# A gated mix of linear attention and a dense squared-ReLU block on one core: low weight parts kept in DRAM, sums moved between engines, and a new table of slots

## The chip, the cores and the metric

The kernel runs on one core of one Trainium2 chip. A core has a matrix engine (TensorE; PE for its matmuls and PEld for its weight loads in the profile), VectorE (DVE), ScalarE (ACT), GpSimd (POOL) and SyncE (SP), which here issues nearly all DMAs. Each engine works through its own instructions in order and waits at semaphores for the others. The metric is device time in microseconds (us). Before the change the median of three runs is 535.49 us (534.55 to 535.69). The profiled execution took 532.88 us, of which 531.1 us lie between its first and its last instruction (the span).

## The reference

`x` is 2048 x 512, in float32. There are 32 heads of 16 features, and the hidden layer of the dense block has 1792 units.

```
g = sigmoid((x * gate_w).sum(-1))
q, k, v = split(x @ wqkv)                      # 32 heads of 16
pq, pk = q @ w_phi[h], k @ w_phi[h]            # per head
phi = concat(softmax(p), softmax(-p))          # 32 features a head, of pq and of pk
kv, z = phi_k^T @ v, phi_k.sum(rows)
a = ((phi_q @ kv) / (phi_q @ z + 1e-6)) @ wo
r = relu(x @ w1 + b1)
b = (r * r) @ w2 + b2
out = g * a + (1 - g) * b
```

## The kernel before

**Precision.** Each large product is made of three matmuls. An operand is split into a high part `hi` (a copy that ScalarE rounds to a shorter format) and a low part `lo = x - hi` (a subtraction, on VectorE or on GpSimd); `mm3` (lines 72 to 75) adds hi.hi, hi.lo and lo.hi in PSUM. So every operand costs a ScalarE copy and a subtraction before TensorE may read it; both are in `split`, where the copy is line 65 and the subtraction line 68.

**Two sweeps.** The rows of `x` are taken in 4 blocks of 512. The first sweep goes through the blocks with hidden chunks 0 to 6 of the dense block, and in the same time makes K and V and sums them into `kv`. The second sweep goes through the blocks again with hidden chunks 7 to 13, and makes Q, the attention's numerator and the output. One step is one chunk for one block: 12 matmuls "up" (`u`) and 12 "down" (`d`), of 128x512 each. The up product runs two steps ahead of the down product (`LAG = 2`). First-sweep results of the dense block go to DRAM (`part`) and are read back in the second sweep.

**K and V by seven products.** A pair is 256 rows. The product of its rows with [K weights | V weights] is made as a 2 x 2 block product in Winograd's form: seven block products instead of eight (`p1` to `p7`), from sums of the left side (`S1` to `S4`, by `rows_make` on GpSimd) and of the right side (`T1` to `T4`, by `sums_make`, line 237, on GpSimd, once for the whole kernel). There are 8 pairs, two in each block. `w_phi` is folded into the K weights (`fold("k")`, small matmuls of 32x32) and into the Q weights (`fold("q")`) before use. Two PSUM banks serve the seven products: `ps_a` holds `X` (p1 + p2) and then `Z` (p5 + p3), `ps_b` holds `Y` (p6, then p7, then p4 in the same bank). VectorE empties them: `t`, `vext` and `k` on line 538, and the features by two reductions and two subtractions, lines 331 to 334, an exponential on ScalarE (336), a sum (339), a reciprocal (341) and a scaling (345). `do_kv` then multiplies the features with V, head by head (line 354), and adds the result to `kvs` by four additions of 17 rows (line 588).

**What sets the order.** The table `steps` is filled by `at(slot, function, ...)`. Slots 2t and 2t + 1 belong to step t, and the first sweep has slots 0 to 55. A scheduling layer then orders each engine's instructions by the order of the program and by its own idea of when their inputs are ready, with a few hints (`high_priority`, `issue_after`). The DMAs of the SP queue are ordered in the same way, and SP waits at each for its buffer.

**The weights of the dense block in the first sweep.** Chunks 0 to 6 are needed in all four blocks, and there is no room to keep them on chip. So each chunk's `w1` and `w2` tile (128x512, 256 KB) is fetched again for each block into one of four staging buffers (`in`), split into `hi` on ScalarE and `lo` on GpSimd (21 + 21 times from block 1 on), and held in one of three buffers each (`fpool`, `NSTR = 3`). The same four staging buffers take the rows of `x` for the gate (`gate_load`).

**The gate.** For each 128 rows VectorE makes a dot product (line 303), ScalarE an exponential of one column (308), and VectorE four small operations (310 to 313).

Of the kernel before, what the change touches and what calls it, by code (L numbers as in the profile page):

```python
# [16 lines left out]
P = 128  # L17
# [7 lines left out]
LAG = 2  # L25
# [10 lines left out]
def tile_gated_mix(ctx: ExitStack, tc: tile.TileContext, xT, xn, wqT, wkT, wphi, wv, wo, w1, b1, w2, b2, gw, out):  # L36
# [72 lines left out]

    def ready(nm, fc, elo=nc.vector):  # L110
# [57 lines left out]
    xkept = dram.tile([NB, NK, 2, P, SB], F32, name="xkept")  # L168
    kvs = const.tile([P, 2 * P], F32, name="kvs")
    nc.gpsimd.memset(kvs, 0.0)  # L170
    vext = [hold.tile([P, H * VW], F32, tag="vz", name=f"vext{i}") for i in range(NV)]
    heads = lambda v: v.rearrange("p (h v) -> p h v", v=VW)
    for v in vext:
        nc.gpsimd.memset(heads(v)[:, :, DH:VW], 1.0)
    zbc = []
# [34 lines left out]
    def raws(*tags):  # L210
        return [wpool.tile([P, 512], F32, tag=tag, name="fold") for tag in tags]

    def foldq_load():
        load_fold("q", wqT, raws("T40l", "T41h", "T41l", "T10h"))
# [17 lines left out]
    def sums_make(kk, early):  # L232
        k1, k2, v1, v2 = st["w", "k"][kk], st["w", "k"][2 + kk], raw["v", kk], raw["v", 2 + kk]
        t1, t4 = [raw.setdefault((op, kk), row()) for op in ("T1", "T4")] if early else (raw["T1", kk], raw["T4", kk])
        raw["T2", kk], raw["T3", kk] = v2, v1
        for o, x, y in ((t1, v1, k1), (v1, v2, v1)) if early else ((v2, v2, t1), (t4, k2, v2)):
            nc.gpsimd.tensor_tensor(o, x, y, ALU.subtract)
# [61 lines left out]
    def gate_dot(n):  # L299
        t = st["xn", n]  # L300
        lg = st["lg", n] = small.tile([P, 1], F32, tag="lg", name="lg")
        with tc.issue_after(st["low"].ins):
            nc.vector.scalar_tensor_tensor(t, t, 1.0, gwb, op0=ALU.mult, op1=ALU.mult, accum_out=lg)

    def gate_chunk(n):
        e = small.tile([P, 1], F32, tag="ge", name="ge")
        with tc.issue_after(st["act"].ins):
            nc.scalar.activation(e, st["lg", n], AF.Exp, scale=-1.0)
        s = slice(n, n + 1)
        nc.vector.tensor_scalar(inv[:, s], e, 1.0, None, ALU.add)  # L310
        nc.vector.reciprocal(e, inv[:, s])
        nc.vector.tensor_scalar(rest[:, s], e, -1.0, 1.0, ALU.mult, ALU.add)
        nc.vector.tensor_scalar(eps[:, s], inv[:, s], 1e-6, None, ALU.mult)
# [36 lines left out]
    def kv_chunk(n, kvps, phi, v):  # L350
        for i in range(NG):
            for j in range(4):
                h = 8 * (i % 4) + 4 * (i // 4) + j
                nc.tensor.matmul(kvps[32 * j:32 * j + VW, 32 * i:32 * i + 32], v[:, h * VW:(h + 1) * VW],
                                 phi[:, 32 * h:32 * h + 32],
                                 start=(n % 2 == 0 and i == 0), stop=(n % 2 == 1),
                                 skip_group_check=True)
# [116 lines left out]
    def start():  # L474
# [12 lines left out]
        st["wphi"], = raws("T40h")  # L487
        nc.sync.dma_start(st["wphi"], wphi)
        load_fold("k", wkT, raws("T30h", "T30l", "T31h", "T31l"))
# [91 lines left out]
    def do_kv(p):  # L581
# [3 lines left out]
        for j in range(4):  # L585
            s = slice(32 * j, 32 * j + VW)
            with tc.high_priority(offset=AHEAD):
                nc.vector.tensor_tensor(kvs[s, :], kvs[s, :], ps[s, :], ALU.add)
# [13 lines left out]
    def kv_done():  # L602
# [3 lines left out]
        for half in range(2):  # L606
            z = hold.tile([P, H * VW], F32, tag="vz", name=f"z{half}")[:, :D]
# [39 lines left out]
    for nm, fc, s in (("w1", 5, 2), ("w2", 3, 2), ("w1", 6, 4), ("w2", 4, 4), ("w2", 5, 6), ("w2", 6, 8)):  # L647
        at(s, fetch, nm, fc)
    for t in range(NFH, NB * NFH):
        for nm, s in (("w1", 2 * t - 5), ("w2", 2 * t - 2)):  # L650
            at(s - 3, fetch, nm, t % NFH)
            at(s, ready_later, nm, t % NFH, nc.gpsimd)

    for kk in range(2):
        for op, s in (("B11", 3), ("B22", 4), ("B21", 5), ("T2", 6), ("T1", 8), ("T3", 9), ("T4", 10)):
            at(s, operand_ready, op, kk)
    for kk in range(2):
        at(3, sums_make, kk, True)
        at(4, sums_make, kk, False)
    for p, made, split_at in ((0, 2, 3), (1, 3, 12), (2, 12, 15), (3, 16, 20), (4, 24, 26), (5, 30, 32), (6, 36, 38), (7, 40, 42)):  # L660
        at(made, rows_make, p)
        at(split_at, rows_ready, p)
    for p in range(NPAIR):
        s = 8.5 + 5.5 * p
        for f, d in ((p1, 0), (p6, 1), (p2, 1), (p5, 3), (p7, 3), (p4, 4), (p3, 4)):
            at(s + d, f, p)
        at(min(s + 7.5, NB * SL - 3), do_kv, p)
    for b in range(NB):
        for c in range(NC):
            s = b * SL + 3 * c - 5 if b else 7 + c  # L670
            at(s, gate_load, b * NC + c)
            at(s + 3 if b else 9 + c, gate_dot, b * NC + c)
            at(s + 5 if b else 10 + c, gate_chunk, b * NC + c)
        at(b * SL + 16, x_save, b)
        if b < NB - 1:
            at((5, 18, 32)[b], x_fetch, b + 1)
            for k in range(NK):
                at((7, 21, 35)[b] + k // 2, x_ready, b + 1, k)
    base = (NB - 1) * SL
    at(3, foldq_load)  # L680
    at(7, fold, "q")
    at(8, foldq_move)
# [8 lines left out]
    at(NB * SL - 3, kv_done)  # L691
# [28 lines left out]
    for t, (sw, b, i) in enumerate(work_list):  # L720
# [31 lines left out]
        for c in range(NC):  # L752
# [68 lines left out]
```

## Time and profile before

| | |
|---|---|
| median of 3 runs | 535.49 us |
| the profiled execution | 532.88 us |
| its span | 531.1 us |
| PE busy (modelled) | 508.8 us |
| DVE busy | 444.4 us |
| ACT busy | 256.6 us |
| POOL busy | 149.6 us |
| moved by DMA | 70.64 MB |
| the last instruction of the first sweep on PE (`kvt`) | at 277.8 us |

A profile lists, for each engine, how long it was busy and what ended its idle time. "Busy" on PE is modelled: a matmul of 128x512 is shown as about 0.39 us long, but the next one starts 0.23 us after it, so overlapping rows hide short idle times. The arrow `<-` in a row of waits names the engine, the output tile and the line that the waiting instruction was released by.

### The profile page before, as it was taken

To read this page: it belongs to the slowest core of one execution; us is meant where nothing else is said; L and a number is where in the kernel's file an instruction comes from. 1 tells how busy PE (TensorE), PEld (TensorE's weight loads), DVE (VectorE), ACT (ScalarE), POOL (GpSimd) and SP (SyncE) were. 2 spreads that over 40 slices of the span, in tenths; PEclk is the share of its full clock that TensorE was granted. 3 is DMA by queue.
4 is the path that set the end of the run, shared out by engine and by line. 5 is a ranking of instruction groups with operands and counts; after the bars stand their busy time and mean duration, and the time that the engine had idled before them with its cause. 6 is when DMAs were issued, how large, how long until landed. Compare 5 with 4: busy or idle time off the path is not lost.

```text
span 531.1 us, 9626 instructions
## 1 busy us (share of the span) xinstructions
PE 508.8 (96%) x3616; PEld 405.3 (76%) x3616; DVE 444.4 (84%) x704; ACT 256.6 (48%) x446; POOL 149.6 (28%) x125
## 2 busy tenths in 40 slices
PE   9969989999979999899989999999999999999997
PEld 5847867787867878678768887878787878788776
DVE  5898999999698997989899979796779777888723
ACT  6646646564526382546464745353534434343530
POOL 4293324542564242123111112121111020211100
PEclk9997999999999999999999999999999999999999
DMA  8859445426443266623267715312226221023112
GB/s 300 296 199 321 136 130 171 157 74 205 136 141 82 80 201 230 238 66 118 83 179 228 236 52 184 97 38 60 76 53 217 65 91 47 11 92 89 35 26 79
DMA packets 44662, 70.64 MB, mean 133 GB/s; under 512 B 7240, under 2 KB 13640, under 8 KB 44616
## 3 DMA queue, kind: packets, MB, share of 16 engines
q1 hardware_dynamic: 44296, 69.63, 40.9%
q8 instruction: 28, 0.46, 0.3%
q10 hardware_dynamic: 288, 0.39, 0.2%
q14 instruction: 18, 0.15, 0.1%
q0 software_dynamic: 32, 0.01, 0.0%
HBM read 45.88 MB, written 17.83 MB: 120 GB/s over the span
## 4 chain that ended last, share of the span: by engine, by line
PE 62%; issue 13%; DVE 11%; POOL 6%; DMA 5%; ACT 1%; SPq 1%; POOLq 0%; DVEq 0%; ACTq 0%
PE d L73 6%; PE d L75 6%; PE d L74 6%; PE u L73 6%; PE u L74 6%; PE u L75 6%; PE q L73 3%; PE q L75 3%; PE att L75 3%; PE att L73 3%; PE q L74 3%; PE att L74 3%; POOL w2l L68 2%; POOL row L256 2%; DMA in<-in_w 2%
## 5 line engine op out<-in xcount | busy, mean ns | idle before, releaser
L435 ACT ACTIVATE r<-u,b1c 128x512 f32<-128x512 f32 x56 | 38.4, 685 | 122.7 <-PE u L75 122.3
L363 POOL TENSOR_TENSOR ez<-e,z 128x512 f32<-128x512 f32 x32 | 41.4, 1313 | 184.5 <-ACT e L336 162.5
L73 PE MATMUL d<-w2h,hh 128*128 128x512 f32 x160 | 63.7, 398 | 0.7 <-DVE row L768 0.7
L68 POOL TENSOR_TENSOR w1l<-in,w1h 128x512 fp32r<-128x512 f32 x21 | 28.5, 1356 | 124.9 <-ACT w1h L65 106.1
L75 PE MATMUL d<-w2h,hl 128*128 128x512 f32 x160 | 63.2, 395 | 0.0
L74 PE MATMUL d<-w2l,hh 128*128 128x512 f32 x160 | 63.0, 393 | 0.0
L75 PE MATMUL u<-xh,w1l 128*128 128x512 f32 x152 | 60.1, 395 | 2.3 <-DVE w1l L68 1.6
L73 PE MATMUL u<-xh,w1h 128*128 128x512 f32 x152 | 60.6, 399 | 1.0 <-ACT w1h L65 0.9
L74 PE MATMUL u<-xl,w1h 128*128 128x512 f32 x152 | 59.8, 393 | 0.0
L68 DVE TENSOR_TENSOR hl<-r,hh 128x512 fp32r<-128x512 f32 x56 | 48.5, 867 | 13.1 <-ACT hh L65 13.0
L336 ACT ACTIVATE e<-e 128x1024 f32<-128x1024 f32 x32 | 33.9, 1059 | 46.6 <-DVE e L334 46.3
L339 DVE TENSOR_REDUCE sm<-e 128x64 f32<-128x1024 f32 x32 | 38.9, 1216 | 20.3 <-ACT e L336 20.2
L387 ACT ACTIVATE phiT<-tb 32x256 f32<-32x256 f32 x64 | 26.5, 413 | 31.6 <-DVE tb L381 30.9
L73 PEld LDWEIGHTS d<-w2h,hh 128*128 128x128 f32 x160 | 30.3, 189 | 7.9 <-DVE row L768 1.2
L75 PEld LDWEIGHTS u<-xh,w1l 128*128 128x128 f32 x152 | 28.8, 190 | 9.5 <-DVE w1l L68 2.0
L65 ACT ACTIVATE hh<-r 128x512 fp32r<-128x512 f32 x56 | 35.3, 630 | 1.4
L436 ACT ACTIVATE r<-r 128x512 f32<-128x512 f32 x56 | 35.2, 628 | 1.2
L73 PEld LDWEIGHTS u<-xh,w1h 128*128 128x128 f32 x152 | 28.7, 189 | 9.3 <-ACT w1h L65 1.8
L75 PEld LDWEIGHTS d<-w2h,hl 128*128 128x128 f32 x160 | 30.4, 190 | 6.7 <-issue 0.4
L68 POOL TENSOR_TENSOR w2l<-in,w2h 128x512 fp32r<-128x512 f32 x21 | 33.1, 1575 | 8.7 <-issue 8.2
L74 PEld LDWEIGHTS d<-w2l,hh 128*128 128x128 f32 x160 | 30.3, 190 | 6.1
L74 PEld LDWEIGHTS u<-xl,w1h 128*128 128x128 f32 x152 | 28.9, 190 | 5.8
(543 smaller groups left out, 1248.9 us busy)
## 6 DMA issues: line engine op xcount, KB each, us to landing
in<-in_w SPq DMA_DIRECT2D x66, 256.0 KB, 2.8
phiT<-tb SPq DMA_DIRECT2D x192, 32.0 KB, 1.8
xin<-in_xT SPq DMA_DIRECT2D x16, 256.0 KB, 4.6
xkept<-xh SPq DMA_DIRECT2D x16, 256.0 KB, 4.0
xkept<-xl SPq DMA_DIRECT2D x16, 256.0 KB, 4.4
in<-in_xn SPq DMA_DIRECT2D x16, 256.0 KB, 2.8
part<-row SPq DMA_DIRECT2D x16, 256.0 KB, 2.1
xh<-xkept SPq DMA_DIRECT2D x16, 256.0 KB, 4.8
```

The source lines that it names most:

```text
L65: i = nc.scalar.activation(hi, src, AF.Copy)
L68: st["low"] = elo.tensor_tensor(lo, src, hi.bitcast(F32), ALU.subtract)
L73: nc.tensor.matmul(o, ah[:, sa], bh[:, sb], start=first, stop=False, **kw)
L74: nc.tensor.matmul(o, ah[:, sa], bl[:, sb], start=False, stop=False, **kw)
L75: return nc.tensor.matmul(o, al[:, sa], bh[:, sb], start=False, stop=last, **kw)
L256: nc.gpsimd.tensor_tensor(o[i], x, y, op)
L336: nc.scalar.activation(ef, ef, AF.Exp)
L339: nc.vector.tensor_reduce(sm, e3, AX.X, ALU.add)
L363: nc.gpsimd.tensor_tensor(ez[:, hs, :], e3[:, hs, :], zbc[half], ALU.mult)
L387: nc.scalar.activation(dst, src, AF.Copy)
L435: nc.scalar.activation(r, ps, AF.Relu, bias=b1c[:, fc:fc + 1])
L436: nc.scalar.activation(r, r, AF.Square)
```

## The change

It has six parts.

1. **Low parts kept.** In block 0 the low part of each `w1` and `w2` chunk is written to DRAM once it is made (`keep`: 14 DMAs of 256 KB). In blocks 1 to 3, `again` fetches the weights as before and reads the low part back straight into its place (42 DMAs of 256 KB); `again_ready` makes only the high part, on ScalarE. The 42 subtractions on GpSimd are gone. The low part's tile is taken when the DMA is issued, two slots before the high part is made.
2. **Right-hand sums** (`sums_make`, 8 subtractions of 128x512) go from GpSimd to VectorE, one slot later.
3. **wq folded in block 1**: `fold("q")` goes from slot 7 to slot 19; its inputs go to `row` tiles and a staging buffer, where they had gone to weight buffers that were still free.
4. **Bank uses respaced**: `p1` starts at slots 8, 13, 20, 25, 30, 35, 40, 46 where it started at 8, 14, 19, 25, 30, 36, 41, 47; `p3` comes before `p4`, which goes one slot further back. `do_kv` is 8 slots after `p1`.
5. **One addition into kvs**: `do_kv`'s matmuls take 32 columns of V instead of 17, so that they fill whole groups of 32 rows, and one addition of 128x256 replaces four of 17x256 (the additional rows are not used). `vext` gets 15 more columns, of zeros at its end.
6. **Gate by blocks**: one chain of exponential and four small operations on 4 columns per block, where there was one on 1 column per 128 rows; the loads and dots have other slots. The writes of `part` in blocks 0 to 2 are put one to two slots later into the program. `rows_make` and `x_fetch` get other slots too.

```
+    def keep(nm, fc):
+        nc.sync.dma_start(lkept[fc, int(nm == "w2")], (up_w if nm == "w1" else down_w)[fc][1].bitcast(F32))
+    def again(nm, fc):
+        fetch(nm, fc)
+        hi, lo = raw[nm, fc, "hl"] = ffn_tiles(nm, fc)
+        nc.sync.dma_start(lo.bitcast(F32), lkept[fc, int(nm == "w2")])
+    def again_ready(nm, fc):
+        hi, lo = raw.pop((nm, fc, "hl"))
+        with tc.issue_after(st["act"].ins):
+            nc.scalar.activation(hi, raw.pop((nm, fc)), AF.Copy)
...
     def foldq_load():
-        load_fold("q", wqT, raws("T40l", "T41h", "T41l", "T10h"))
+        load_fold("q", wqT, [row() for _ in range(NK)])
+        st["wphi"] = load(wphi)
...
-            nc.gpsimd.tensor_tensor(o, x, y, ALU.subtract)
+            nc.vector.tensor_tensor(o, x, y, ALU.subtract)
...
-                nc.tensor.matmul(kvps[32 * j:32 * j + VW, 32 * i:32 * i + 32], v[:, h * VW:(h + 1) * VW],
+                nc.tensor.matmul(kvps[32 * j:32 * j + 32, 32 * i:32 * i + 32], v[:, h * VW:h * VW + 32],
...
-        for j in range(4):
-            s = slice(32 * j, 32 * j + VW)
-            with tc.high_priority(offset=AHEAD):
-                nc.vector.tensor_tensor(kvs[s, :], kvs[s, :], ps[s, :], ALU.add)
+        with tc.high_priority(offset=AHEAD):
+            nc.vector.tensor_tensor(kvs, kvs, ps, ALU.add)
...
+    for fc in range(NFH):
+        at(max(2 * (fc - LAG), 1) + 1, keep, "w1", fc)
+        at(2 * fc + 1, keep, "w2", fc)
     for t in range(NFH, NB * NFH):
-        for nm, s in (("w1", 2 * t - 5), ("w2", 2 * t - 2)):
-            at(s - 3, fetch, nm, t % NFH)
-            at(s, ready_later, nm, t % NFH, nc.gpsimd)
+        at(2 * t - 8, again, "w1", t % NFH)
+        at(2 * t - 6, again_ready, "w1", t % NFH)
+        at(2 * t - 4, again, "w2", t % NFH)
+        at(2 * t - 2, again_ready, "w2", t % NFH)
...
-        for op, s in (("B11", 3), ("B22", 4), ("B21", 5), ("T2", 6), ("T1", 8), ("T3", 9), ("T4", 10)):
+        for op, s in (("B11", 4), ("B22", 5), ("T2", 6), ("B21", 6), ("T1", 7), ("T3", 8), ("T4", 9)):
...
-    for p in range(NPAIR):
-        s = 8.5 + 5.5 * p
-        for f, d in ((p1, 0), (p6, 1), (p2, 1), (p5, 3), (p7, 3), (p4, 4), (p3, 4)):
+    at(16, foldq_load)
+    at(19, fold, "q")
+    at(20, foldq_move)
+    for p, s in enumerate((8, 13.5, 20, 25.2, 30.4, 35.6, 40.8, 46)):
+        for f, d in ((p1, 0), (p6, 1), (p2, 1), (p5, 3), (p7, 3), (p3, 4), (p4, 5)):
             at(s + d, f, p)
-        at(min(s + 7.5, NB * SL - 3), do_kv, p)
+        at(min(s + 8, NB * SL - 2), do_kv, p)
...
+            elif sw == 0 and b < NB - 1:
+                at(2 * t + 3 + c // 2, lambda *a: nc.sync.dma_start(*a), dst, o)
```

The next lines show what the table makes of three places. They are the scheduled rows of one engine; the numbers behind names are tile numbers of each build, and nothing in them is a time.

**VectorE at the start, in step 1**, around the transposes of the folded K weights (`wkin<-foldk`). `w1l` is the low part of a chunk of w1. Before:

```order
L68 TENSOR_TENSOR w1l_231<-in,w1h_230 128x512
L68 TENSOR_TENSOR hl<-r,hh 128x512
L68 TENSOR_TENSOR w2l_255<-in,w2h_254 128x512
L68 TENSOR_TENSOR w1l_359<-in,w1h_358 128x512
L68 TENSOR_TENSOR w2l_363<-in,w2h_362 128x512
L68 TENSOR_TENSOR S0ol_384<-row,S0oh_382 128x512
L68 TENSOR_TENSOR S0ol_385<-row,S0oh_383 128x512
L206 STREAM_TRANSPOSE wkin<-foldk_285 128x4x4x32
L206 STREAM_TRANSPOSE wkin<-foldk_286 128x4x4x32
L206 STREAM_TRANSPOSE wkin<-foldk 128x4x4x32 x2
L68 TENSOR_TENSOR B110l<-wkin,B110h 128x512
```

and with the change:

```order
L68 TENSOR_TENSOR w2l_258<-in,w2h_257 128x512
L68 TENSOR_TENSOR w2l_370<-in,w2h_369 128x512
L68 TENSOR_TENSOR S0ol_377<-row,S0oh_375 128x512
L68 TENSOR_TENSOR S0ol_378<-row,S0oh_376 128x512
L222 STREAM_TRANSPOSE wkin<-foldk_292 128x4x4x32
L222 STREAM_TRANSPOSE wkin<-foldk_293 128x4x4x32
L222 STREAM_TRANSPOSE wkin<-foldk 128x4x4x32 x2
L68 TENSOR_TENSOR w1l_234<-in,w1h_233 128x512
L68 TENSOR_TENSOR w1l_366<-in,w1h_365 128x512
L251 TENSOR_TENSOR row<-wvin,wkin 128x512 x2
L251 TENSOR_TENSOR wvin<-wvin 128x512 x2
```

The low parts of w1 chunks 3 and 4 have moved behind the transposes, and the sums of line 251 now stand in VectorE's queue.

**VectorE at the end of a pair** (pair 4 of 0 to 7). `k` is the bank Y emptied after p4, `mx`, `mn` and `e` read it, and `vext<-kz` empties bank Z after p3, which p1 of the next pair waits for. Before:

```order
L538 TENSOR_TENSOR k_2160<-ky,t_1922 128x512
L331 TENSOR_REDUCE mx<-k_2160 128x32
L332 TENSOR_REDUCE mn<-k_2160 128x32
L333 TENSOR_TENSOR e<-k_2160,mx 128x32x16
L334 TENSOR_TENSOR e<-mn,k_2160 128x32x16
L538 TENSOR_TENSOR vext_113<-kz,t_1965 128x32x16
L339 TENSOR_REDUCE sm<-e 128x64
```

and with the change:

```order
L68 TENSOR_TENSOR xl_0_2129<-xin,xh_0_2128 128x512
L68 TENSOR_TENSOR xl_1_2133<-xin,xh_1_2132 128x512
L555 TENSOR_TENSOR vext_114<-kz,t_1932 128x32x16
L555 TENSOR_TENSOR k_2162<-ky,t_1892 128x512
L68 TENSOR_TENSOR hl<-r,hh 128x512
L347 TENSOR_REDUCE mx<-k_2162 128x32
L348 TENSOR_REDUCE mn<-k_2162 128x32
```

`vext<-kz` has moved from behind the four feature operations to ahead of them and of `k`.

**The SP queue at the start**, from the first DMA behind the V weights (`wvin`) on; `in<-in_w` fetches a weight chunk. Before:

```order
L641 DMA gwb<-in_gw 128x512
L83 DMA in<-in_w 128x512 x2
L182 DMA fold<-in_wqT 128x512 x4
L83 DMA in<-in_w 128x512 x2
L642 DMA b2b<-in_b 128x512
```

and with the change:

```order
L111 DMA lkept<-w2l_200 128x512
L656 DMA gwb<-in_gw 128x512
L83 DMA in<-in_w 128x512 x2
L111 DMA lkept<-w1l_224 128x512
L111 DMA lkept<-w1l_184 128x512
L111 DMA lkept<-w1l_189 128x512
L111 DMA lkept<-w2l_258 128x512
L111 DMA lkept<-w2l_370 128x512
```

The loads of the Q weights are gone from this place and writes of low parts stand there. The first `in<-in_w` goes into the staging buffer of w1 chunk 3, so it is issued once the subtraction `w1l_234` above is done.

More of the change, by code (lines that the diff above doesn't have):

```diff
@@ L168, in tile_gated_mix @@
     xkept = dram.tile([NB, NK, 2, P, SB], F32, name="xkept")
+    lkept = dram.tile([NFH, 2, P, 512], F32, name="lkept")
     kvs = const.tile([P, 2 * P], F32, name="kvs")
     nc.gpsimd.memset(kvs, 0.0)
-    vext = [hold.tile([P, H * VW], F32, tag="vz", name=f"vext{i}") for i in range(NV)]
-    heads = lambda v: v.rearrange("p (h v) -> p h v", v=VW)
+    vext = [hold.tile([P, H * VW + 32 - VW], F32, tag="vz", name=f"vext{i}") for i in range(NV)]
+    heads = lambda v: v[:, :H * VW].rearrange("p (h v) -> p h v", v=VW)
     for v in vext:
         nc.gpsimd.memset(heads(v)[:, :, DH:VW], 1.0)
+        nc.gpsimd.memset(v[:, H * VW:], 0.0)
     zbc = []
@@ L486, in start @@
         fetch("w2", 1)
-        st["wphi"], = raws("T40h")
-        nc.sync.dma_start(st["wphi"], wphi)
-        load_fold("k", wkT, raws("T30h", "T30l", "T31h", "T31l"))
+        t = [wpool.tile([P, 512], F32, tag=tag, name="fold") for tag in ("T40h", "T30h", "T30l", "T31h", "T31l")]
+        st["wphi"] = t[0]
+        nc.sync.dma_start(t[0], wphi)
+        load_fold("k", wkT, t[1:])
         fetch("w1", 4)
```

42 lines of the change are left out of this document (20 added, 22 removed).

## The prediction

> **What bounds the kernel now.** I read the page first.
>
> ```profile
> span 531.1 us, 9626 instructions
> PE 508.8 (96%) x3616; PEld 405.3 (76%) x3616; DVE 444.4 (84%) x704; ACT 256.6 (48%) x446; POOL 149.6 (28%) x125
> ```
>
> TensorE looks full, but its busy time is modelled. So next comes the table of windows, cut at stages: the start, the rest of block 0, blocks 1, 2 and 3 of the first sweep, and the second sweep. The columns after the window are its length and the busy time of PE, PEld, DVE, ACT and POOL, then the granted clock, the DMA share and GB/s.
>
> ```profile
> 0.00:38.10 38.10, 34.57 (x251) 23.56 (x251) 29.26 (x32) 23.64 (x40) 21.26 (x26) 1.00 0.76 260
> 38.10:88.00 49.90, 45.96 (x421) 36.25 (x421) 46.23 (x87) 30.52 (x55) 18.26 (x15) 0.90 0.62 203
> 88.00:150.00 62.00, 59.78 (x505) 48.46 (x504) 55.98 (x91) 30.14 (x52) 27.83 (x23) 1.00 0.46 144
> 150.00:214.00 64.00, 58.79 (x499) 47.06 (x497) 56.86 (x97) 30.26 (x52) 25.46 (x20) 1.00 0.45 150
> 214.00:278.00 64.00, 59.97 (x626) 48.07 (x626) 59.07 (x98) 34.99 (x61) 15.44 (x11) 1.00 0.42 132
> 278.00:531.10 253.10, 249.69 (x1320) 201.89 (x1318) 196.99 (x305) 107.07 (x188) 41.35 (x32) 1.00 0.30 93
> ```
>
> In the second sweep PE has no holes up to the tail, and VectorE is busy 197 of 253 us. In the first sweep VectorE is busy 89 to 93% of every stage behind the start: there the two engines are nearly equal, and PE waits. The view of waits, for PE alone (total us, times, longest), names all of its waits but the one at launch:
>
> ```profile
> PE ky L73 <- DVE vext L538: 4.3, 3, 2.2
> PE kx L73 <- DVE vext L538: 4.2, 3, 1.8
> PE foldq L191 <- ACT r L435: 3.4, 1, 3.4
> PE u L75 <- DVE w1l L68: 1.6, 1, 1.6
> PE kvps L354 <- DVE rest L312: 1.4, 1, 1.4
> PE u L73 <- ACT w1h L65: 0.9, 1, 0.9
> PE d L73 <- DVE row L768: 0.7, 1, 0.7
> PE ky L73 <- DVE rest L312: 0.7, 1, 0.7
> PE u L75 <- POOL w1l L68: 0.6, 1, 0.6
> PE kvt L612 <- DVE kvs L588: 0.2, 1, 0.2
> ```
>
> They add up to 18.0 us. Each of the 14 waits hides a little more, since a matmul is shown 0.39 us long while the next starts 0.23 us after it:
>
> ```profile
> 215.02 0.39 PE L75 MATMUL kx<-B110h,xl 128*128 128x512 f32 x1
> 215.25 0.40 PE L73 MATMUL kx<-B111h,xh 128*128 128x512 f32 x1
> ```
>
> That is 14 x 0.16 = 2.2 us. Then there is the clock:
>
> ```profile
> 40.00:43.00 3.00, 2.45 (x126) 2.12 (x126) 2.63 (x3) 2.94 (x6) 0.93 (x1) 0.50 1.00 369
> 43.00:46.40 3.40, 3.40 (x28) 2.26 (x8) 3.40 (x7) 2.98 (x6) 0.73 (x1) 0.50 0.64 140
> 75.00:80.00 5.00, 4.38 (x13) 3.13 (x14) 5.00 (x12) 1.00 (x3) 2.84 (x2) 0.71 0.42 107
> ```
>
> PE is busy 5.85 us at 0.50, which loses 2.9 us, and 5.0 x 0.29 = 1.45 us go at 75. So what PE loses in the first sweep is 18.0 + 2.2 + 4.35 = 24.6 us. No change of waits alone can gain more.
>
> **The change part by part.** Why is VectorE late? One reason is GpSimd: the first row is a subtraction beside a GpSimd one (last row, second fence), the second the same form 8 us later with GpSimd idle.
>
> ```profile
> 34.67 1.78 DVE L68 TENSOR_TENSOR B210l<-wkin,B210h 128x512 fp32r<-128x512 f32 x1
> 42.46 0.68 DVE L68 TENSOR_TENSOR w1l<-in,w1h 128x512 fp32r<-128x512 f32 x1
> ```
>
> ```profile
> 34.16 1.74 POOL L237 TENSOR_TENSOR wvin<-wvin,row 128x512 f32<-128x512 f32 x1
> ```
>
> So a GpSimd subtraction costs VectorE up to 1.1 us; as others may fall into idle time I take 0.8. (The Trainium skill, "SBUF — State Buffer", section "SBUF: two separate sides", says that the two share a port pair which one of them holds for its whole instruction while the other blocks. By that rule each of the 50 GpSimd subtractions that go could have cost its whole length, 1.74 us in the row above and near 87 us in all, and VectorE would have far more room than I count; the rows show 1.1 us at most, and I hold to them.)
>
> Other rows that the sums need, of the view by lines, and two of the chain of waits (start, us; the Q fold's twin at full clock, and one `do_kv`):
>
> ```profile
> L588 DVE TENSOR_TENSOR kvs<-kvs,kvps 17x256 f32<-17x256 f32 x32 | 13.3, 415 | 0.3
> L206 DVE STREAM_TRANSPOSE wkin<-foldk 128x512 f32<-128x512 f32 x4 | 2.5, 680 | 0.0
> L311 DVE RECIPROCAL ge<-inv 128x1 f32<-128x1 f32 x16 | 2.4, 153 | 0.2
> L354 PEld LDWEIGHTS kvps<-e,vext 128*17 128x17 f32 x1024 | 9.3, 96 | 4.6 <-issue 2.5 <-ACT r L436 1.8 <-ACT w2h L65 0.4
> L400 PEld LDWEIGHTS num<-phiT,kvb 64*32 64x32 f32 x256 | 3.9, 106 | 3.8 <-ACT e L336 1.8 <-issue 1.1
> L191 PEld LDWEIGHTS foldq<-fold 32*32 32x32 f32 x128 | 2.2, 135 | 4.4 <-ACT r L435 3.8 <-issue 0.4
> ```
>
> ```profile
> 17.45 1.83 PE foldk L191 x102
> 112.43 1.20 PE kvps L354 x82
> ```
>
> *The start* (to 46.4 us). ACT stood waiting for the GpSimd sums, its ReLU came late, and the Q fold waited 3.4 us for a PSUM buffer; then the clock fell. Sums on VectorE take 8 x 0.68 = 5.4 us, less than what GpSimd's eight took from it (8 x 0.8 = 6.4), and the fold leaves this place. The waits of 3.4 and 1.6, two restarts (0.3) and the clock (2.9) go: 8.2. New: w1 chunk 3's low part stands behind the four transposes (2.5 us), and its up product may wait. The bounds are 0 and 2.5; I take 0.5, since VectorE reaches the transposes two subtractions sooner. Queued behind it is SP, whose next weight fetch wants that staging buffer. Net -7.7 (-5 to -8.2).
>
> *The rest of block 0.* Lost before: 0.9 + 0.6 + 0.7, three restarts and the clock's 1.45, together 4.15. VectorE's 29.26 + 46.23 = 75.5 us to 88 us become: less 15 GpSimd subtractions x 0.8 = 12, plus 5.4 for the sums, less 2.5 (Q transposes, later), 1.25 (three of four `kvs` additions) and 1.7 (three gate chains of four operations near 0.15): 63.5. PE needs 88 less its losses of 12.4 and less the fold (1.8): 74. As VectorE starts some 6 us in and also waits for inputs, 63.5 of 68 leaves little room: I keep 4 us of stalls in place of 4.15, now for VectorE's features and block ends. Net -0.2 (-4.15 to +4).
>
> *The banks* (pairs 1 to 7): 4.3 + 4.2 + 0.7 and seven restarts, 10.3 us. The worst kind, at 212 us on VectorE:
>
> ```profile
> 209.97 0.69 DVE L303 SCALAR_TENSOR_TENSOR in<-in,gwb 128x512 f32<-128x512 f32 x1 [3.38 <-issue]
> 210.59 0.69 DVE L538 TENSOR_TENSOR k<-ky,t 128x512 f32<-128x512 f32 x1
> 213.71 0.68 DVE L538 TENSOR_TENSOR vext<-kz,t 128x512 f32<-128x512 f32 x1
> ```
>
> The gate's dot held the queue 3.4 us, and bank Z was emptied only 3.1 us after `k`'s start, behind the features. Now `vext<-kz` precedes `k`, and PE has 12 + 6 matmuls x 0.23 = 4.1 us between p3's end and the next p1, where the shortest spacing was 2.8. For Y, p7 to p4 is 30 matmuls (6.9 us), not 12. VectorE also loses work here: per block 2.5 us of `kvs`, 1.7 of gates, some 14 x 0.8 = 11 of GpSimd's holds. I leave 1.5 us of waits, for dots that wait for their rows as here. Net -8.8 (-5 to -10.3).
>
> *The end of the sweep*: 1.4 + 0.2 and two restarts, 1.9. `do_kv` is a slot later, and the second sweep's first low parts still stand before `k`: 1.2 stays, net -0.7 (-1.9 to +1). `kv_done` is two slots later; the z loads and GpSimd's product come before the first numerator, many steps on: nothing, or 2 us at most if VectorE's sum over that product blocks its queue.
>
> *The Q fold in block 1.* Its matmuls count on both sides. It holds both up buffers and both banks until VectorE's transposes are through, behind a pair's features. Bounds: 0 (hidden behind 12 down matmuls, 2.8 us) and 4 (more than the 3.4 it waited before); I take 1.6, nearer the low end as ACT is no longer blocked.
>
> *Weights of 32 columns.* Loads of 17 columns take 96 ns; of 32 columns 106 (`num`), or 135 (`foldq`, at half clock). So 8 bursts x 1.20 x 0.10 = 1.0; bounds 0 and 3.9.
>
> *The clock.* At 75 us it fell behind waits of 0.9 and 0.6 us. One more such dip would cost 1.45; with fewer waits, I take 0.8 (0 to 3). (The Trainium skill, "TensorE: Matmul & The Clock Gate", section "What's actually happening", puts the drop behind an idle window of about 3.4 us. The 3.42 us at the fold agrees; the dip at 75 us does not. By the rule this term would be 0 and the sum 0.8 us better.)
>
> *Low parts by DMA.* On GpSimd they cost PE only the 0.6 above, and VectorE its time; `SPq L83 <- POOL` below is their price on the queue.
>
> ```profile
> SPq L83 <- POOL w1l L68: 70.2, 20, 10.3
> ```
>
> ```profile
> in<-in_w SPq DMA_DIRECT2D x66, 256.0 KB, 2.8
> xh<-xkept SPq DMA_DIRECT2D x16, 256.0 KB, 4.8
> ```
>
> Now SP waits for PE instead: a reread for chunk t is issued once chunk t-3's products are done. Until its own use lie two steps, 48 matmuls or 11.0 us, and landing takes 4.8 us by the nearest row (a reread from DRAM): 6 us to spare. Behind it on SP wait fetches, gate rows and `xkept` writes. The 56 transfers add 14.7 MB to 70.6; with the DMA share at 0.62 and less in the first sweep but for the start, I count nothing.
>
> Sum: -7.7 - 0.2 - 8.8 - 0.7 + 1.6 + 1.0 + 0.8 = -14.0. The span becomes 517.1, the profiled execution 518.9. That execution lies 2.6 us under the median of the runs; taken from the median it gives **521.5 us**.
>
> **The rivals.** (a) *Nearly every wait goes*: block 0 has no VectorE stalls and the clock holds, gain 18 to 24 us, 514.5. For it: GpSimd's holds may be worth more than 0.8 each. Against: 63.5 of 68 in block 0. (b) *The start is crowded*: SP stands some 8 us for w1 chunk 3's low part, then writes, rows of `x` and weights come at once; the window from 40 us already ran at DMA share 1.00 and 369 GB/s, so 256 KB take 0.7 us and 40 such transfers 28 us. If weights come late for two or three steps by 2 to 3 us, 7 go: 528.5. Against: the Q weights' 2 MB in and out leave the start. (c) *Slower: the reread is late in every step*, because SP, in order, is held by a gate row or an x write for more than the 6 us to spare. From 0.7 us a step (14/21) on it outweighs the gain; at 1.5 us over 21 steps it costs 31: 552. For it: gate dots held SP before. Against: those holds came with GpSimd's. (d) *VectorE is not relieved*: GpSimd's holds fell into idle time, the sums add 5.4, and waits stay: 534 to 537.
>
> **How the numbers follow.** Forecast (gain 10 to 18) 0.50, (a) 0.21, (b) 0.18, (c) 0.06, (d) 0.05. The range is 510.5 (just under every loss gone, 510.9) to 531 ((b) in full); (c) and (d) are left out. A difference of 0.2% is what can be told from none; slower takes (c) and 0.02 of (d), the same 0.02, so faster 0.90.
>
> **What would show it.** `foldq` no longer waits near 37 us and the clock stays at 1.0 there; POOL busy falls from 150 to about 75 us (50 subtractions near 1.5); the mean of `hl` on VectorE falls under 0.75; eight `kvs` additions of 128x256 near 0.42 us; waits of kx and ky under 2 us. If PE waits for `w1l<-lkept` or for ACT `w1h`, (b) or (c) holds; if `hl` stays long without GpSimd, (d). The second sweep must stay within 1 us of 253; if not, the reasoning is wrong.

## The result, and the profile after

The changed kernel takes 516.16 us (median of 4 runs, 514.65 to 519.11) where the kernel before takes 535.02 us (4 runs, 533.35 to 535.69): a ratio of 0.9659, 95% interval 0.9608 to 0.9709. The profiled execution took 515.52 us with a span of 513.8 us, so 17.3 us less than the span before. The prediction was 521.5 us, within 510.5 to 531.

The page of the changed kernel, its span and busy times:

```profile
span 513.8 us, 9521 instructions
...
PE 503.5 (98%) x3616; PEld 404.0 (79%) x3616; DVE 404.1 (79%) x640; ACT 254.6 (50%) x434; POOL 73.6 (14%) x77
```

VectorE has lost 40 us of busy time and GpSimd 76. The table of windows, with the cuts of the prediction (length, PE, PEld, DVE, ACT, POOL, granted clock, DMA share, GB/s):

```profile
0.00:38.10 38.10, 35.75 (x258) 25.08 (x259) 26.71 (x39) 25.19 (x44) 10.89 (x21) 1.00 0.91 321
38.10:88.00 49.90, 48.27 (x332) 38.97 (x331) 43.92 (x76) 31.26 (x54) 7.97 (x8) 1.00 0.91 303
88.00:150.00 62.00, 59.21 (x619) 47.59 (x618) 45.86 (x76) 29.68 (x49) 6.49 (x8) 1.00 0.64 208
150.00:214.00 64.00, 64.00 (x647) 52.42 (x646) 52.52 (x84) 36.32 (x59) 6.52 (x8) 1.00 0.64 206
214.00:278.00 64.00, 64.00 (x528) 52.74 (x527) 53.11 (x89) 34.26 (x56) 3.00 (x2) 1.00 0.59 193
```

PE has no hole left in blocks 2 and 3, and the clock stays at 1.00. The view of waits names all that is left on PE but the launch:

```profile
PE u L73 <- DVE wqin L222: 2.3, 1, 2.3
PE u L75 <- DVE w1l L68: 1.4, 1, 1.4
PE kz L73 <- DVE e L350: 1.3, 1, 1.3
...
PE kx L73 <- DVE wqin L222: 0.5, 1, 0.5
PE d L73 <- DVE row L786: 0.2, 1, 0.2
```

That is 5.7 us where it was 18.0. No wait of kx or ky for `vext` is among them, nor one for the rereads. SP now waits for PE and ScalarE, no longer for GpSimd:

```profile
SPq L116 <- PE u L75: 34.0, 14, 5.2
SPq L83 <- ACT w2h L121: 32.1, 16, 4.9
```

The gain lies in the first sweep. The first numerator product of the second sweep starts 17.9 us earlier, and from there to the end both kernels take about the same (209.4 us before, 210.0 us now). The view of the tile `num`, before and then after (shortest, median and longest in ns, then first and last start):

```profile
L400 PE MATMUL num<-phiT,kvb x256: 375/376/401, 321.7 to 513.4; 64*32 64x256 f32 x128
```

```profile
L416 PE MATMUL num<-phiT,kvb x256: 373/376/401, 303.8 to 496.0; 64*32 64x256 f32 x128
```

### The profile page after: what moved, and what is told of

It is laid out like the page before. It is cut to its first block, busy times and chain, and to the rows that moved or that the text cites. A ratio compares the mean times of both kernels' runs of the same rounds, so it can differ in the third digit from the quotient of the medians.

```text
span 513.8 us, 9521 instructions
## 1 busy us (share of the span) xinstructions
PE 503.5 (98%) x3616; PEld 404.0 (79%) x3616; DVE 404.1 (79%) x640; ACT 254.6 (50%) x434; POOL 73.6 (14%) x77
## 2 busy tenths in 40 slices
DMA packets 52869, 85.58 MB, mean 167 GB/s; under 512 B 8152, under 2 KB 14552, under 8 KB 52824
## 4 chain that ended last, share of the span: by engine, by line
PE 82%; DVE 7%; DMA 5%; ACT 4%; issue 1%; SPq 1%; DVEq 0%; ACTq 0%
PE u L73 8%; PE d L73 8%; PE d L74 8%; PE d L75 8%; PE u L75 8%; PE u L74 8%; PE q L73 3%; PE q L75 3%; PE q L74 3%; PE att L73 3%; PE att L75 3%; PE att L74 3%; PE kvps L370 2%; PE num L416 2%; PE ky L73 2%; PE ky L74 2%
## 5 line engine op out<-in xcount | busy, mean ns | idle before, releaser
L73 PE MATMUL d<-w2h,hh 128*128 128x512 f32 x160 | 62.8, 393 | 0.2 <-DVE row L786 0.2
L73 PE MATMUL u<-xh,w1h 128*128 128x512 f32 x152 | 59.9, 394 | 2.5 <-DVE wqin L222 2.3
L68 DVE TENSOR_TENSOR hl<-r,hh 128x512 fp32r<-128x512 f32 x56 | 38.6, 689 | 18.3 <-ACT hh L65 18.3
L73 PEld LDWEIGHTS u<-xh,w1h 128*128 128x128 f32 x152 | 28.5, 188 | 10.5 <-DVE wqin L222 2.8
L65 ACT ACTIVATE hh<-r 128x512 fp32r<-128x512 f32 x56 | 35.3, 631 | 1.6
L73 PEld LDWEIGHTS d<-w2h,hh 128*128 128x128 f32 x160 | 30.0, 188 | 7.5 <-DVE row L786 0.7
L270 POOL TENSOR_TENSOR row<-xin 128x256 f32<-128x256 f32 x16 | 16.0, 1006 | 123.5 <-DVE S4ol L68 32.7
L381 DVE TENSOR_REDUCE dz<-ez 128x64 f32<-128x1024 f32 x16 | 19.4, 1211 | 9.4 <-POOL ez L379 9.3
```

What stands on the lines that cost most here:

```text
L65: i = nc.scalar.activation(hi, src, AF.Copy)
L68: st["low"] = elo.tensor_tensor(lo, src, hi.bitcast(F32), ALU.subtract)
L73: nc.tensor.matmul(o, ah[:, sa], bh[:, sb], start=first, stop=False, **kw)
L381: nc.vector.tensor_reduce(dz, ez, AX.X, ALU.add)
```

## The experiments

Twelve kernels were run, in three groups; the runs of the kernel before were taken on the same chip for each group (medians 532.78, 533.19 and 534.47 us), so the ratio is what compares across groups.

| run | median, us | ratio to before (95%) | profiled span, us |
|---|---|---|---|
| the change | 516.16 | 0.9659 (0.9608 to 0.9709) | 513.8 |
| low parts on GpSimd, old slots | 528.34 | 0.9898 (0.9846 to 0.9951) | 528.0 |
| low parts on VectorE, old slots | 526.32 | 0.9867 (0.9824 to 0.9910) | 525.2 |
| sums on GpSimd | 519.87 | 0.9751 (0.9706 to 0.9797) | 518.1 |
| old bank slots | 517.72 | 0.9712 (0.9666 to 0.9758) | 515.5 |
| 42 more operations on VectorE | 516.83 | 0.9676 (0.9632 to 0.9719) | 515.8 |
| staging held by VectorE | 516.65 | 0.9685 (0.9644 to 0.9725) | 514.5 |
| reread twice | 518.76 | 0.9717 (0.9675 to 0.9759) | 517.8 |
| 17 columns, four additions | 518.17 | 0.9712 (0.9666 to 0.9758) | 514.8 |
| low parts on VectorE, the change's slots | 514.98 | 0.9647 (0.9621 to 0.9672) | 512.9 |
| low parts on GpSimd, the change's slots | 527.31 | 0.9877 (0.9852 to 0.9902) | 526.0 |
| three slots moved | 513.87 | 0.9630 (0.9601 to 0.9658) | 512.2 |
| before, with the rereads alone | 519.83 | 0.9734 (0.9708 to 0.9759) | 517.1 |

**Undoing one part at a time.** First the low parts, back on GpSimd, without stores and rereads:

```
-        at(2 * t - 8, again, "w1", t % NFH)
...
+        for nm, s in (("w1", 2 * t - 5), ("w2", 2 * t - 2)):
+            at(s - 3, fetch, nm, t % NFH)
+            at(s, ready_later, nm, t % NFH, nc.gpsimd)
```

> The changed kernel, but the low parts of the FFN weights of blocks 1 to 3 are again subtracted on GpSimd (42 instructions, with the fetches where the kernel before had them) and are neither stored nor reread; sums, banks, fold and gates stay as changed. Theory (VectorE's time is what was short, and each GpSimd subtraction takes up to 1.1 us, about 0.8, of it): VectorE loses 42 x 0.8 = 34 us, some 11 a block, on top of 46 to 53 busy of 62 to 64; it is full again, SP waits for GpSimd near 70 us again, and PE waits of 4 to 9 us come back: 520 to 526 against the change's 516.2. Rival (the new spacing of the banks did it; GpSimd's holds fell into idle time): 515.5 to 517.5, PE waits still near 6 us.

528.34 us, more than either side expected. This part carries the most: 0.0239 of 535 us is 12.8 us. SP waits for GpSimd again (`w1l` alone 71.8 us), but VectorE is not full: it was busy 46.71 of 62 us in block 1. So the direction was right, and the reason given for it was already in doubt.

The same with `nc.vector` in place of `nc.gpsimd`:

> The changed kernel, but the low parts of blocks 1 to 3 are subtracted on VectorE itself (42 more instructions near 0.68 us), neither stored nor reread. Theory (VectorE's time, whoever takes it): 42 x 0.68 = 28.6 us, some 9.5 a block, so blocks 2 and 3 stand at 62 of 64 us and PE waits 3 to 8 us more: 519 to 524. Rival 1 (it was GpSimd: its slow subtractions held the staging buffers and so SP, and stretched VectorE; any quick engine would do): 515.5 to 517.5. Rival 2 (the DMA traffic of the reread costs something): under 515.

526.32 us, beyond the first theory's range, and nothing like the rivals: another engine in the same slots did not clearly help (1.7 us by the ratio, with intervals that overlap).

The sums back on GpSimd (`nc.gpsimd.tensor_tensor` in `sums_make`):

> The changed kernel, but the eight subtractions that make the right-hand sums in block 0 are on GpSimd again. Theory (ACT waited for them, its ReLU came late, PE waited and the clock fell): ACT waits for GpSimd again for 2 to 4 us near 30 to 40 us, PE loses 2 to 6 us there and perhaps half clock: 518 to 522. Rival (the loss at the start came from the Q fold, which stood behind that ReLU, and the fold has left): within 1 us of 516.2.

The theory holds, with 4.3 us more span (the intervals of the two ratios just overlap). ScalarE's timeline shows it waiting at the high parts of T20 and T21 for GpSimd, with the ReLU's second half (line 452) queued behind the second one:

```profile
36.98 0.63 ACT L65 ACTIVATE T20h<-wvin 128x512 fp32r<-128x512 f32 x1 [1.19 <-POOL wvin L251]
37.52 0.67 ACT L451 ACTIVATE r<-u,b1c 128x512 f32<-128x512 f32 x1
40.38 0.63 ACT L65 ACTIVATE T21h<-wvin 128x512 fp32r<-128x512 f32 x1 [2.18 <-POOL wvin L251]
40.91 0.61 ACT L452 ACTIVATE r<-r 128x512 f32<-128x512 f32 x1
```

`w1h` is queued behind that, and PE waited 2.6 us for it (`PE u L73 <- ACT w1h L65: 2.6, 1, 2.6` in the waits). With the sums on VectorE that wait is not there.

The old table of bank slots:

> The changed kernel, but the pairs' products, do_kv and the left-hand sums stand in the slots of the kernel before (p4 ahead of p3, one start every 5.5 slots, do_kv 7.5 slots behind). Theory (spacing and relief share the 10.3 us of bank waits): kx and ky wait for vext again, with a VectorE that is less busy 0.5 to 1.5 us each in place of 1.5 to 2.2: 3 to 7 us, 519 to 523. Rival 1 (the relief of VectorE did it alone): under 1.5 us, 516 to 517.7. Rival 2 (spacing did it alone): all 10 us come back, 526.

The two measures differ. The median, 517.72 us, stands at the edge of rival 1, but the kernel before was faster in this group, and by the ratio the old slots cost 2.8 us (0.0053 of 535), near the theory's lower bound of 3. The intervals of the ratios overlap, and the span is 1.7 us longer. The waits speak for rival 1: PE waited once for `vext`, 0.8 us:

```profile
PE kx L73 <- DVE vext L555: 0.8, 1, 0.8
```

So the respacing, on which the prediction had leaned for the banks, is worth some 2 to 3 us once the low parts are off GpSimd, which these runs cannot tell from nothing.

**What did the low parts cost?** Two additions to the changed kernel part VectorE's time from its hold on the staging buffers. The first adds time only:

```
+            nc.vector.tensor_reduce(junk, hi.bitcast(F32).rearrange("p (h f) -> p h f", f=DH), AX.X, ALU.max)
```

> The changed kernel, rereads and all, with 42 added reductions on VectorE (128x512, near 0.68 us each) that read the high part of a chunk once ScalarE has made it; the staging buffers are not touched by them, and what they write is not used. Theory 1 (VectorE's own time is what the low parts cost): as with the low parts on VectorE, 8 to 12 us more than the change, a ratio to the kernel before of 0.980 to 0.990, with PE waits for VectorE near 10 us in the first sweep. Theory 2 (what cost was the hold: a staging buffer stays taken until the low part is made, SP waits, and the weights and rows behind it come late): at most 3 us more, a ratio of 0.966 to 0.971.

The second holds the staging buffer and takes next to no time:

```
+            nc.vector.tensor_tensor(junk, t[:, :1], hi[:, :1].bitcast(F32), ALU.subtract)
```

> The changed kernel, rereads and all, with 42 added subtractions of 128x1 on VectorE (0.06 to 0.15 us each, some 4 us in all) that read the staged chunk and its high part, so that the staging buffer stays taken until VectorE has come to them; what they write is not used. Theory 1 (VectorE's own time): at most 3 us more than the change, a ratio to the kernel before of 0.966 to 0.971. Theory 2 (the hold of the staging buffers, and SP with them): SP waits for VectorE some 60 us, and 8 to 12 us more, a ratio of 0.980 to 0.990.

Neither costs anything that these runs can tell. With the added reductions (42 near 0.67 us) VectorE is busy 429.7 us in place of 404.1, and the ratio is 0.9676, 0.9 us more; PE's waits add up to 7.7 us in the profiled execution, against 5.7. So VectorE's busy time, taken alone, is not what is short. The hold gives 0.9685; but SP waited only 31 us at these subtractions, not 60, so it was a weaker hold than meant.

That left the slots. The next two runs take the slots of the change for fetch and split, without DRAM, first on VectorE:

```
+        at(2 * t - 8, fetch, "w1", t % NFH)
+        at(2 * t - 6, ready_later, "w1", t % NFH)
+        at(2 * t - 4, fetch, "w2", t % NFH)
+        at(2 * t - 2, ready_later, "w2", t % NFH)
```

> As the run with the low parts on VectorE, no stores, no rereads, but each chunk is fetched and split in the slots of the change: w1 at 2t-8 and 2t-6, w2 at 2t-4 and 2t-2, so that it lies two slots in a staging buffer, not three. Two chunks a step then take 2 of the 4 staging buffers and not 3, with the gate's rows beside them. Theory (neither VectorE's time nor its touch of the buffer cost anything by itself; what cost 11 us was that staging was full and SP, in order, late with all that stands behind it): SP's waits for VectorE's low parts fall from 97 us to under 50, and the ratio to the kernel before is 0.966 to 0.975. Rival (what counts is that a product has to wait for a low part made in VectorE's queue, or that all three costs come together): 0.982 to 0.990, as before.

and then on GpSimd (`ready_later, ..., nc.gpsimd`):

> The same slots, with the low parts on GpSimd. Theory (full staging): the time falls with SP's waits, ratio 0.968 to 0.978, some 2 us behind VectorE's version, as GpSimd's subtractions of 1.4 to 1.7 us hold the buffers longer. Rival (GpSimd itself, by what it takes from VectorE): stays at 0.985 to 0.995.

VectorE's version is as fast as the change, with nothing stored or reread (70.89 MB moved, not 85.58). GpSimd's is 12.3 us slower in the same group of runs, inside its rival's range, and the engine of 42 subtractions is the only difference in what is written. But the reason in the expectation fell: SP waits longer than with the old slots, and still the time is low. The queue's waits of VectorE's version, then of GpSimd's:

```profile
SPq L83 <- DVE w2l L68: 81.7, 26, 15.4
SPq L83 <- DVE w1l L68: 24.1, 23, 6.8
```

```profile
SPq L83 <- POOL w2l L68: 75.0, 18, 9.7
SPq L83 <- POOL w1l L68: 25.3, 19, 3.9
```

106 us against 100. Nor is it VectorE's load. In the fast version VectorE does all the work itself and is busy 49.78 of 49.90 us in the rest of block 0 and 60.06 of 64 in block 2, and PE has no hole of note there:

```profile
38.10:88.00 49.90, 49.51 (x337) 39.87 (x335) 49.78 (x84) 28.89 (x50) 9.94 (x8) 1.00 0.57 190
...
150.00:214.00 64.00, 64.00 (x647) 52.38 (x646) 60.06 (x95) 34.50 (x57) 7.96 (x8) 1.00 0.48 156
```

What does differ is where VectorE stands still. The groups of `hl` and of the gate's dot from 88 to 278 us (busy, mean ns of one | idle time just before them and what ended it), VectorE's version first:

```profile
L68 DVE TENSOR_TENSOR hl<-r,hh 128x512 fp32r<-128x512 f32 x19 | 13.2, 695 | 2.0 <-ACT hh L65 2.0
...
L318 DVE SCALAR_TENSOR_TENSOR in<-in,gwb 128x512 f32<-128x512 f32 x11 | 7.4, 677 | 0.0
```

```profile
L68 DVE TENSOR_TENSOR hl<-r,hh 128x512 fp32r<-128x512 f32 x18 | 16.6, 924 | 1.9 <-ACT hh L65 1.9
...
L318 DVE SCALAR_TENSOR_TENSOR in<-in,gwb 128x512 f32<-128x512 f32 x11 | 9.1, 826 | 11.7 <-DMA in<-in_xn 7.0 <-issue 3.2 <-DMA row<-wqm 1.5
```

With GpSimd in it, the dot, in order, holds VectorE 11.7 us, 7.0 of them for the gate's late rows; operations beside a GpSimd one are stretched as well. One of these holds can be followed into PE. The features behind the dot come late, and `do_kv` waits for them:

```profile
159.93 0.75 DVE L318 SCALAR_TENSOR_TENSOR in<-in,gwb 128x512 f32<-128x512 f32 x1 [4.83 <-DMA in<-in_xn]
...
170.71 1.08 PE L370 MATMUL kvps<-e,vext 128*32 128x32 f32 x64 [3.40 <-DVE e L361]
```

From 169 to 175 us PE then ran at a clock of 0.72 (4.29 busy x 0.28 = 1.2), so this one late row goes with 4.6 of the 12.3 us. PE waited at no low part of the weights in this run. With VectorE alone the row was there each time; SP then waits for the very engine that will need the row, which may be why. How the rest of the 12.3 us divides between late rows and stretched operations was not tried.

The two VectorE versions, old and new slots, differ by 0.022 of 535, or 11.8 us. In the old slots the Q fold's transposes stand behind two low parts and two splits of `x` on VectorE:

```profile
97.69 1.23 DVE L68 TENSOR_TENSOR w1l<-in,w1h 128x512 fp32r<-128x512 f32 x1
98.84 1.21 DVE L68 TENSOR_TENSOR w2l<-in,w2h 128x512 fp32r<-128x512 f32 x1
99.97 1.81 DVE L68 TENSOR_TENSOR xl<-xin,xh 128x512 fp32r<-128x512 f32 x2
101.70 1.90 DVE L222 STREAM_TRANSPOSE wqin<-foldq 128x512 f32<-128x512 f32 x3
```

PE waited 3.8 us there and then ran at a clock of 0.67 for 5 us (4.45 busy x 0.33 = 1.5). In the new slots they go before the low parts,

```profile
94.20 2.44 DVE L222 STREAM_TRANSPOSE wqin<-foldq 128x512 f32<-128x512 f32 x4
...
97.68 0.68 DVE L68 TENSOR_TENSOR w2l<-in,w2h 128x512 fp32r<-128x512 f32 x1
```

and PE waited 0.7 us for them. So 4.6 of the 11.8 us go with the order in VectorE's queue. Three other waits in the old slots (for `w1h`, `inv` and `dz`) are 1.6 to 2.0 us each, where the new slots have one of 1.3 for `w1h`, and behind the wait for `dz` the clock fell again (0.83 from 310 to 320 us). Which of the four slots matters was not tried.

**The DMA's room.** Every reread issued twice:

```
+        nc.sync.dma_start(hi.bitcast(F32), lkept[fc, int(nm == "w2")])
         nc.sync.dma_start(lo.bitcast(F32), lkept[fc, int(nm == "w2")])
```

> The changed kernel with every reread issued twice: the kept low part goes first into the buffer of the high part, which ScalarE then writes as before, and then into its own; 42 x 256 KB = 11 MB more on SP's queue. Theory (the reread has 6 us to spare of its two steps, and the DMA engines have room): within 1 us of the change, a ratio to the kernel before of 0.964 to 0.968, and no PE wait for the rereads. Rival (the transfers are near their limit, SP's order or the DMA share): from 0.2 us a step on, 4 us and more, a ratio over 0.973, with PE waits for ScalarE's high parts or the rereads.

Between the two: a span 4.0 us longer, and intervals that overlap. PE never waited for a reread. But a gate row landed late, VectorE stood 5.76 us at its dot, the features and the Q fold's transposes followed, and PE waited 4.9 us for these, not 2.3:

```profile
91.16 0.69 DVE L319 SCALAR_TENSOR_TENSOR in<-in,gwb 128x512 f32<-128x512 f32 x1 [5.76 <-DMA in<-in_xn]
...
100.75 2.50 DVE L223 STREAM_TRANSPOSE wqin<-foldq 128x512 f32<-128x512 f32 x4
```

Here the price of the traffic is paid by the row that an in-order engine waits for, not by the transfer that is added.

**The small part.** 17 columns and four additions again:

> The changed kernel, but the products of `do_kv` load 17 columns again in place of 32, and `kvs` is summed in four additions of 17x256 instead of one of 128x256. Theory (a load of 32 columns lasts 109 ns, one of 17 columns 96): each burst is 0.15 us shorter, 1.0 us over eight, and VectorE's 8 x (4 x 0.415 - 0.40) = 10 us more fall into its idle time: 0 to 1.2 us faster than the change, a ratio to the kernel before of 0.963 to 0.966. Rival (VectorE's time is dear even now): 2 to 4 us slower, a ratio of 0.970 to 0.974.

Neither is clear: the ratio lies in the rival's range, but its interval overlaps the change's, and the span is only 1.0 us longer. The bursts themselves are 0.03 us apart: 1.20 us here, and in the change's chain of waits (start, us)

```profile
161.13 1.23 PE kvps L370 x82
```

**One part alone.** The kernel before with `keep`, `again` and `again_ready` added:

> The kernel before with the stores and rereads of the low parts alone: sums on GpSimd, old banks, the Q fold at the start, old gates and `kvs`. Theory (undoing this part cost the most of all, so it carries most of the gain by itself; the waits for vext fall with it): 8 to 12 us faster than before, a ratio of 0.977 to 0.985, with the Q fold's wait of 3.4 us and its half clock still there. Rival (the parts need each other: without the new spacing and the sums the waits for vext stay): under 5 us, a ratio over 0.990.

It gains more than expected, 14.2 us by the ratio (0.0266 of 535), of the change's 18.2. Its waits on PE:

```profile
PE u L75 <- DVE w1l L68: 3.6, 2, 2.2
PE u L73 <- DVE wqin L221: 2.4, 1, 2.4
PE kx L73 <- DVE vext L553: 1.6, 2, 1.2
```

The waits of kx and ky for `vext`, 8.5 us before, are 1.6 in the old bank slots. Most of what the change gains beyond it lies in the start, where the sums and the Q fold are as before: the waits of the first two rows all fall within the first 48 us.

**A version against the waits that are left:**

```
+    at(0, keep, "w1", 1)
...
-            s = b * SL + 2 * c if b else 7 + c
+            s = b * SL + 2 * c + (3 if b == 1 and c else 0) if b else 7 + c
...
-                at((7, 20, 34)[b] + k // 2, x_ready, b + 1, k)
+                at((7, 21, 34)[b] + k // 2, x_ready, b + 1, k)
```

> The change with three slots moved, against the waits that its trace still shows: the low part of w1 chunk 1 is stored at once, so that chunk 3's low part can be made ahead of the K fold's transposes; the gate's rows of block 1 after the first are loaded and multiplied three slots later, and the x of block 2 is split one slot later, so that neither stands before the Q fold's transposes on VectorE. Theory (the waits of 1.4 us at 22 us and of 2.3 and 0.5 us at 96 to 100 us go, with three restarts): 3 to 5 us off the change, a ratio to the kernel before of 0.956 to 0.961. Rival (the transposes still come late, behind a pair's features, or the wait comes back elsewhere): 0.963 to 0.968.

513.87 us; the ratio, 0.9630, stands at the lower edge of the rival's range. Its span is 1.6 us shorter than the change's; the intervals overlap, so that it is faster than the change is not shown by the times. The waits moved as meant, in part, and one came back elsewhere, as the rival had it:

```profile
PE d L73 <- DVE row L788: 1.5, 1, 1.5
PE kz L73 <- DVE e L350: 1.3, 1, 1.3
PE u L73 <- DVE wqin L222: 1.1, 1, 1.1
...
PE kx L73 <- DVE wqin L222: 0.7, 1, 0.7
```

The wait for `w1l` is gone, but `d` at the end of block 0 waits 1.5 us in place of 0.2: there the dot held VectorE 2.9 us for a gate row, 2.0 in the change. The fold's waits fell from 2.8 to 1.8 us, and the granted clock was 1.000 in 5 of 6 executions, against 1 of 4 of the change.

## Why the prediction was right, and where it was not

The time fell inside the range and on the right side, 5.3 us under the point. The point is nearer than its terms deserve: the start and the Q fold fell short by 2.6 us together, and the other five went 6.4 us the other way. Place by place, from the waits, with 0.16 us for each restart as in the prediction:

| term | predicted, us | profiled execution, us |
|---|---|---|
| start (8.2 lost before) | -7.7 | -6.6 (1.4 and a restart left) |
| rest of block 0 (4.15) | -0.2 | -2.3 (0.25 + 1.3 and two restarts left) |
| banks (10.3) | -8.8 | -10.3 |
| end of the sweep (1.9) | -0.7 | -1.9 |
| Q fold in block 1 | +1.6 | +3.1 (2.3 + 0.5 and two restarts) |
| 32 columns | +1.0 | +0.25 (8 x 0.03) |
| clock | +0.8 | 0 |
| sum | -14.0 | -17.75; the span fell by 17.3 |

One of the losses was read too large from its row: in the window from 75 to 80 us PE was busy 4.38 us, not 5.0, so the clock cost 1.3 us there and not 1.45. It changes nothing else.

**The step that failed is VectorE's budget.** The prediction kept 4 us of stalls in block 0 because "63.5 of 68 leaves little room", and 1.5 and 1.2 us at the banks and the end for the same cause. In the change itself VectorE was busy 26.71 + 43.92 = 70.6 us up to 88 us, 7 more than the 63.5 (PE was also further along by then), and PE's stalls in the rest of block 0 came to 1.9 us. Two runs put 26 us more work on VectorE, up to 49.78 of 49.90 us, and PE's waits were 7.7 and 4.7 us, against 5.7 in the change. So with GpSimd out of the way VectorE's time is not what is short; what the rows show instead are instructions at which VectorE itself stands and waits. In its own rows the prediction had the better lead: the dot that "held the queue 3.4 us", and `SPq L83 <- POOL`, 70.2 us, which it called a price on the queue and then gave no term of its own. From 88 to 278 us the dots held VectorE 6.0 us in the kernel before, and 0.0 in the same kernel with the rereads added. That this, and not the stretched operations, made the waits of the kernel before is inferred, not shown; one such chain from row to PE is shown above, in the run with GpSimd in the new slots.

**GpSimd's price** was taken as 0.8 us of VectorE for each subtraction. With the low parts on GpSimd, VectorE's 640 operations take 423.7 and 425.5 us in place of 404.1: 19.6 and 21.4 us over 42, so 0.47 to 0.51 each. For the eight sums it is 1.0: 406.7 us with eight operations of 0.68 us fewer, so 8.0 us. The size was fair on the whole (why the two engines stretch each other is in the last section); but as much time of VectorE's own, added alone, cost nothing that the runs can tell.

**The banks** were right in sum, and their reason only half. The prediction set out the new order of `vext` and `k` and the new distances first. In the old slots the waits for `vext` are 0.8 us with the rest of the change, and 1.6 with the rereads alone.

**The start** was mis-sized, 0.5 where 1.4 us are left. The four transposes were counted; that the low part's tile was still being stored was not:

```profile
23.54 0.69 DVE L68 TENSOR_TENSOR w1l<-in,w1h 128x512 fp32r<-128x512 f32 x1 [0.52 <-DMA lkept<-w1l]
```

The stores, priced as traffic, also hold the tile that they read.

**The Q fold** cost 3.1, nearer its upper bound of 4 than the 1.6 taken. VectorE stood 2.95 us at a gate row, the features came after it, then the transposes:

```profile
88.46 0.69 DVE L318 SCALAR_TENSOR_TENSOR in<-in,gwb 128x512 f32<-128x512 f32 x1 [2.95 <-DMA in<-in_xn]
...
97.76 2.50 DVE L222 STREAM_TRANSPOSE wqin<-foldq 128x512 f32<-128x512 f32 x4
```

**32 columns.** 8 x 1.20 x 0.10 took the load of weights as what sets a burst's pace. A load did grow, from 96 to 109 ns, but the burst grew by 0.03 us and not 0.12.

**The clock** did not dip in the profiled execution, but in three of the four: their mean granted clocks are 1.000, 0.992, 0.997 and 0.997, and 0.003 of 514 us is 1.5 us. The term was fair.

Of the rivals, (c) is answered by the doubled rereads, which PE never waited for; (b) by the waits, in which no fetch of weights stands; (d) by the result. Rival (a) is the nearest: 514.5, two of the four runs lie within 1.1 us of it. By the profiled execution the gain, 17.3 us, is just inside the 10 to 18 of the forecast; by the medians, 18.9 us, it is inside the 18 to 24 of (a), and what (a) said of block 0 and of the clock came nearly true in the profiled execution. It gave as its reason that GpSimd's holds might be worth more than 0.8 us each, and that is not how it came. Of the marks, POOL's busy time (73.6), `hl` (689 ns), eight `kvs` additions (400 ns each) and the second sweep held; `kvt` now stands two slots later, so that its start, named there as the cut, is no measure of the second sweep, and the numerators are.

## What to carry to other kernels

An engine at 90% busy is not yet what bounds; ask at which instruction it stands still and whose data it waits for, and add work to it to see whether its time is short. Look for what a slow helper engine costs through the in-order queues that wait for it, too: a DMA queue held by it can bring late rows to an engine that has nothing else to do with it. Before moving data through DRAM to spare an engine, try the same slots without it: here the version without stores and rereads is as fast.

## What the runs showed of the hardware

Whether the clock falls behind a wait does not follow from its length alone. Behind waits of 2.33 and 0.46 us it stayed at 1.00 in the profiled execution of the change; behind 2.16 and 0.46 us in the run with the sums on GpSimd it fell:

```profile
102.00:105.00 3.00, 2.54 (x9) 1.76 (x8) 2.56 (x5) 0.00 (x0) 0.00 (x0) 0.67 1.02 366
105.00:108.00 3.00, 3.00 (x11) 2.17 (x9) 0.00 (x0) 0.60 (x1) 0.00 (x0) 0.76 0.90 343
```

(The Trainium skill, "TensorE: Matmul & The Clock Gate", section "What's actually happening", puts the drop behind an idle window of about 3.4 us. Neither wait of this run was that long.)

VectorE and GpSimd take turns, but only where a VectorE operation reads two operands from on-chip memory (SBUF), as a subtraction `lo = x - hi` does. In the run with the low parts on GpSimd in the new slots:

```profile
151.59 1.29 POOL L68 TENSOR_TENSOR w2l<-in,w2h 128x512 fp32r<-128x512 f32 x1 [0.76 <-ACT w2h L65]
151.92 1.52 DVE L68 TENSOR_TENSOR hl<-r,hh 128x512 fp32r<-128x512 f32 x1
152.84 1.73 POOL L68 TENSOR_TENSOR w1l<-in,w1h 128x512 fp32r<-128x512 f32 x1
```

`hl` ends at 153.44 us, 0.56 behind the end of GpSimd's first subtraction (152.88), and GpSimd's second ends 1.13 us behind `hl`. With nothing beside them the two forms take 0.68 and about 1.27 us, so each waited for the other and then did its work. The prediction's row of 1.78 us is the same: it ends 0.55 us behind the GpSimd row shown with it, whose 1.74 us hold a wait of GpSimd's own. In the first sweep of the kernel before, reductions and operations with one operand in PSUM kept 0.69 us or less beside GpSimd. The 0.47 to 0.51 us for each subtraction are a mean over all 42, whether or not VectorE had an operation of the kind to do beside them. (The Trainium skill, "SBUF — State Buffer", section "SBUF: two separate sides", has whichever starts first, GpSimd or a VectorE operation with two SBUF inputs, take the shared ports for its whole instruction while the other blocks; these rows agree.)
